# KV sums as row-pair matmuls into two PSUM banks, in a one-core gated attention and MLP kernel

## The chip, the cores and the metric

The kernel runs on one core of one Trainium2 chip. The metric is device time in microseconds, lower is better. Times are medians over single executions. The profile is of one execution, and its span is about 2 us shorter than the time measured for the same execution. Kernels are compared only within the same rounds.

## The reference, cut to what matters

```python
# x: (1, 2048, 448), bf16; 16 heads of 28
q, k, v = split(x @ wqkv)                        # per head
phi_k = concat(softmax(k @ w_phi), softmax(-(k @ w_phi)))   # phi_q likewise
kv  = einsum("bhsf,bhsd->bhfd", phi_k, v)        # the KV sums: over all 2048 tokens
z   = einsum("bhsf->bhf", phi_k)
a   = ((phi_q @ kv) / (phi_q @ z + 1e-6)) @ wo
b   = gelu(x @ w1 + b1) @ w2 + b2
out = g * a + (1 - g) * b                        # g = sigmoid(x . gate_w)
```

The change concerns `kv` and `z`: one sum over all tokens for eight pairs of heads.

## The kernel before

It is one program without loops; TensorE goes through projections, the hidden layer of the MLP (`hp`), in whose midst the KV sums (`acc`) are put, then the attention's numerators (`nm`) and the output layer (`y`). The sums are 128 matmuls, each over 128 tokens with 58 moving columns (columns of the operand that streams through the array), all summed in one bank of PSUM, the memory that matmuls write:

```python
    def kv_sum(acc, u):
        for t in (2 * u, 2 * u + 1):
            for x in range(NPR):                       # 8 pairs of heads
                nc.tensor.matmul(acc[:, 0, x * (PW + 2):(x + 1) * (PW + 2)],   # 58 columns
                                 lhsT=phik[:, t, x, :, :].rearrange("p s w -> p (s w)"),
                                 rhs=vaug[:, t, x, :], start=(t == 0 and x == 0),
                                 stop=(t == NT - 1), skip_group_check=True)

    def kv_out(acc):
        nc.vector.tensor_tensor(out=KV[:], in0=acc[...], in1=mask[...], op=ALU.mult)   # cut

    for n in range(2 * NJ):                            # 28 units of the hidden layer
        m_unit(n // NJ, n % NJ)                        # 14 matmuls, 64 rows each, in row pairs
        if n < 8:
            q_norm(n)                                  # VectorE sums, GpSimd multiplies, SP transposes
        # ... loads of b2 (n == 5) and w2 (n == 8), cut
        if n == 4:
            acc = wide("acc")
            for u in range(8):
                kv_sum(acc, u)
            kv_out(acc)
            gates()
```

A matmul that reads partitions 0 to 63 uses the upper half of the array's rows, one that reads 64 to 127 the lower half, and two such can run at once: in the trace the two matmuls of such a pair start 4 ns apart. `m_unit` is written that way; `kv_sum` is not.

The softmax here doesn't subtract the row's maximum and nothing guards it: scores larger than these inputs give would overflow.

## Time and profile before

| | before |
|---|---|
| time, median (range), 3 runs | 149.19 us (149.14 to 149.22) |
| span of the profile | 147.5 us |
| TensorE busy | 143.4 us |
| first hp matmul to first nm matmul, by their starts | 46.25 us |

The lines of the page and of the views that carry the argument stand in the prediction.

### The profile page before, as it was taken

The page shows a single profiled execution, that of the slowest core. Times are in us where ns is not written, and L with a number is a line of the kernel's source. Part 1 is how long each engine was busy: PE and PEld are TensorE (multiplying, and loading weights), DVE is VectorE, ACT ScalarE, POOL GpSimd, SP SyncE. Part 2 cuts the span into 40 slices and gives each one's busy share as a digit, 9 for nine tenths or more (in the row PEclk, how much of TensorE's full clock was granted, in tenths as well). Part 3 has the DMA queues.
Part 4 walks back from the last instruction along what each step waited for, and adds up shares of the span by engine and source line. Part 5 has one row for each costly group of instructions (what it writes and reads, how often), then busy time and mean ns, then how long its engine had stood idle before and what let it go on. Part 6 is the DMA issues. An engine that isn't in the chain of part 4 may idle for free.

```text
span 147.5 us, 3138 instructions
## 1 busy us (share of the span) xinstructions
PE 143.4 (97%) x1302; PEld 75.0 (51%) x1302; DVE 87.9 (60%) x139; ACT 75.2 (51%) x91; POOL 68.4 (46%) x49
## 2 busy tenths in 40 slices
PE   7999999999999999999999999999999999999992
PEld 2665544555544854444444445554555455555462
DVE  2353699999999999999300017765665245550312
ACT  1654999989889436767677774000621021111100
POOL 7999999899977999919950000000000000000000
PEclk9999999999999999999999999999999999999999
DMA  4999999999700089982999913333433012225011
GB/s 142 227 215 193 168 195 222 218 220 214 160 2 2 4 144 131 226 169 47 126 158 201 351 66 71 71 76 73 129 98 76 31 62 67 67 67 71 31 62 31
DMA packets 44928, 18.02 MB, mean 122 GB/s; under 512 B 36785, under 2 KB 44914, under 8 KB 44914
## 3 DMA queue, kind: packets, MB, share of 16 engines
q1 hardware_dynamic: 43698, 17.16, 56.5%
q10 hardware_dynamic: 1152, 0.65, 1.6%
q8 instruction: 10, 0.16, 0.5%
q14 instruction: 4, 0.03, 0.1%
q0 software_dynamic: 64, 0.01, 0.0%
HBM read 6.28 MB, written 1.84 MB: 55 GB/s over the span
## 4 chain that ended last, share of the span: by engine, by line
PE 91%; DMA 4%; SPq 2%; DVE 1%; issue 0%
PE y L515 29%; PE hp L463 29%; PE pq L346 7%; PE y L520 6%; DMA WqT<-in_A_wqkv_dram 4%; PE v_ps L330 4%; PE pk L338 4%; PE pk L231 3%; PE acc L353 3%; PE nm L476 3%; SPq L146 2%; PE v_ps L231 2%; PE y L525 1%; PE w_ps L262 1%; PE pk L218 1%; SPq L134 1%
## 5 line engine op out<-in xcount | busy, mean ns | idle before, releaser
L515 PE MATMUL y<-w_sb,gel 128*128 128x448 bf16 (+2 forms) x238 | 45.2, 342 | 0.0
L463 PE MATMUL hp<-xT,w_sb 64*128 64x512 bf16 x196 | 42.6, 376 | 0.0
L463 PE MATMUL hp<-xS,w_sb 64*128 64x512 bf16 x196 | 42.6, 376 | 0.0
L468 ACT ACTIVATE gel<-hp,b1T 128x1024 bf16<-128x1024 f32 x28 | 30.8, 1110 | 13.2 <-PE hp L463 13.2
L515 PEld LDWEIGHTS <-gel 128*128 128x128 bf16 x238 | 22.3, 98 | 20.0 <-issue 0.9
L538 ACT ACTIVATE b2u<-b_sb,ungate 128x448 f32<-128x448 bf16 x16 | 10.2, 666 | 40.8 <-DVE res L530 40.8
L463 PEld LDWEIGHTS <-w_sb 64*128 64x128 bf16 x392 | 19.0, 94 | 23.0
L306 POOL TENSOR_TENSOR phik<-phik,rec 128x1792 bf16<-128x1792 bf16 (+1 forms) x8 | 24.9, 3126 | 1.8 <-DVE rec L303 1.7
L480 DVE TENSOR_SCALAR den<-nm,einv 128x16 f32<-128x16 f32 x16 | 3.7, 230 | 27.9 <-PE nm L476 27.9
L530 DVE SCALAR_TENSOR_TENSOR res<-y,ungate,b2u 128x448 bf16<-128x448 f32 (+2 forms) x17 | 10.8, 653 | 15.4 <-PE y L525 10.1
L301 DVE TENSOR_REDUCE sums<-phik 128x64 f32<-128x1792 bf16 x8 | 16.0, 2000 | 3.2 <-ACT phik L292 3.2
L306 POOL TENSOR_TENSOR oT<-oT,rec 128x1792 bf16<-128x1792 bf16 x4 | 12.7, 3212 | 1.1 <-DVE rec L303 1.1
L520 PE MATMUL y<-wo_sb,oT 128*128 128x448 bf16 (+2 forms) x51 | 11.7, 341 | 0.0
L346 PE MATMUL pq<-Wpq,xT 64*128 64x448 bf16 x56 | 11.5, 349 | 0.0
L346 PE MATMUL pq<-WqS,xS 64*128 64x448 bf16 x56 | 11.4, 349 | 0.0
L306 POOL TENSOR_TENSOR w_sb<-w_sb,rec 128x1792 bf16<-128x1792 bf16 x3 | 9.6, 3212 | 3.0 <-DVE rec L303 3.0
L483 DVE TENSOR_TENSOR o_tok<-nm,den 128x448 bf16<-128x448 f32 x16 | 10.0, 624 | 0.6
L303 DVE RECIPROCAL rec<-sums 128x64 f32<-128x64 f32 x16 | 8.8, 553 | 1.4
L200 DVE CAST vaug<-v_ps 128x896 bf16<-128x896 f32 x7 | 7.5, 1071 | 2.0 <-PE v_ps L212 1.6
L291 ACT ACTIVATE phik<-pk 128x896 bf16<-128x896 f32 x8 | 7.6, 947 | 1.9 <-PE pk L220 1.9
L301 DVE TENSOR_REDUCE sums<-oT 128x64 f32<-128x1792 bf16 x4 | 7.9, 1981 | 0.0
L292 ACT ACTIVATE phik<-pk 128x896 bf16<-128x896 f32 x8 | 7.7, 958 | 0.0
(113 smaller groups left out, 173.6 us busy)
## 6 DMA issues: line engine op xcount, KB each, us to landing
w_sb<-in_B_w_dram SPq DMA_DIRECT2D x4, 784.0 KB, 11.5
out_dram<-res SPq DMA_DIRECT2D x15, 112.0 KB, 1.8
w_sb<-in_B_w_dram SPq DMA_DIRECT2D x2, 448.0 KB, 4.8
w_sb<-in_B_w_dram SPq DMA_DIRECT2D x2, 336.0 KB, 3.7
xS<-xT SPq DMA_DIRECT2D x2, 256.0 KB, 3.5
EqT<-in_A_x_dram ACTq DMA_DIRECT2D x1, 448.0 KB, 3.2
xS<-xT SPq DMA_DIRECT2D x2, 192.0 KB, 3.5
wo_sb<-in_A_wo_dram SPq DMA_DIRECT2D x1, 336.0 KB, 16.9
```

The source lines that it names most:

```text
L292: nc.scalar.activation(out=dst[:, :, :, 1, 0:PW], in_=src, func=ACT.Exp, scale=-1.0)
L301: nc.vector.reduce_sum(out=sums[:], in_=ph, axis=AX.X)
L303: nc.vector.reciprocal(out=rec[:], in_=sums[:])
L306: eng.tensor_tensor(out=ph[:, lo:hi], in0=ph[:, lo:hi], in1=rec[:, lo:hi, :, None].to_broadcast([P, hi - lo, 2, DH]), op=ALU.mult)
L346: nc.tensor.matmul(pq[:, i, 0:D], lhsT=x_half(i, k, h)[:, r * P:(r + 1) * P], rhs=w_half(Wpq, WqS, i, k), start=(k == 0), stop=(k == NK - 1))
L463: nc.tensor.matmul(hp[:, i, :], lhsT=w1_sb[i * HP:(i + 1) * HP, k, j * P:(j + 1) * P], rhs=x_half(i, k, h), start=(k == 0), stop=(k == NK ...
L468: nc.scalar.activation(out=gel[h][:, j, :], in_=hp[:].rearrange("p a b -> p (a b)"), func=ACT.Gelu_apprx_tanh, bias=b1T[:, j:j + 1])
L483: nc.vector.tensor_tensor(out=o_tok[:, t % 4, 0:D].rearrange("p (x h d) -> p x h d", x=NPR, h=2), in0=nmv[:, :, 0:PW].rearrange("p x (h d) ...
L515: nc.tensor.matmul(y, lhsT=gel[t // 8][:, j, (t % 8) * P:(t % 8 + 1) * P], rhs=w2_sb[:, j, cols], start=(opens and j == 0), stop=False)
L520: nc.tensor.matmul(y, lhsT=oT[:, c, t * P:(t + 1) * P], rhs=wo_sb[:, c, cols], start=False, stop=(closes and c == 2))
L530: nc.vector.scalar_tensor_tensor(out=res[:, cols], in0=y, scalar=ungate[:, t:t + 1], in1=b2u[t][:, cols], op0=ALU.mult, op1=ALU.add)
L538: nc.scalar.activation(out=b2u[t][:], in_=b2_sb[:], func=ACT.Copy, scale=ungate[:, t:t + 1])
```

## The change

Intent: the sums get the same 64-row shape as their neighbours, so that TensorE no longer changes its tiling (how its rows are divided among matmuls), and the halves, each in a bank of its own, are added by VectorE. To make room for `total`, `b2u` loses a buffer. Separately a small load on GpSimd moves ahead of three small operations.

```diff
+    nc.gpsimd.dma_start(wphi[0:64, 3, :], wphi_rows[384:448, :])
     nc.gpsimd.memset(hmask[:], 1.0)
     ... two affine_select on hmask ...
-    nc.gpsimd.dma_start(wphi[0:64, 3, :], wphi_rows[384:448, :])
@@ kv_sum
-                nc.tensor.matmul(acc[:, 0, x * (PW + 2):(x + 1) * (PW + 2)],
-                                 lhsT=phik[:, t, x, :, :]..., rhs=vaug[:, t, x, :], ...)
+                for i in range(2):
+                    rows = slice(i * HP, (i + 1) * HP)
+                    nc.tensor.matmul(acc[:, i, x * (PW + 2):(x + 1) * (PW + 2)],
+                                     lhsT=phik[rows, t, x, :, :]..., rhs=vaug[rows, t, x, :], ...)
@@ kv_out
+        halves = [acc[:, i, 0:NPR * (PW + 2)] for i in range(2)]
+        total = work.tile([P, NPR * (PW + 2)], F32, name="total", bufs=1)
+        nc.vector.tensor_copy(out=total[:], in_=halves[0])
+        nc.vector.tensor_tensor(out=total[:], in0=total[:], in1=halves[1], op=ALU.add)
         nc.vector.tensor_tensor(
-            out=KV[:], in0=acc[:, 0, ...],
+            out=KV[:], in0=total[:]...,
@@ b2_tile
-        b2u[t] = work.tile([P, D], F32, name="b2u", bufs=3)
+        b2u[t] = work.tile([P, D], F32, name="b2u", bufs=2)
```

More of the change, by code (lines that the diff above doesn't have):

```diff
@@ L352, in kv_sum @@
             for x in range(NPR):
-                nc.tensor.matmul(acc[:, 0, x * (PW + 2):(x + 1) * (PW + 2)],
-                                 lhsT=phik[:, t, x, :, :].rearrange("p s w -> p (s w)"),
-                                 rhs=vaug[:, t, x, :], start=(t == 0 and x == 0),
-                                 stop=(t == NT - 1), skip_group_check=True)
+                for i in range(2):
+                    rows = slice(i * HP, (i + 1) * HP)
+                    nc.tensor.matmul(acc[:, i, x * (PW + 2):(x + 1) * (PW + 2)],
+                                     lhsT=phik[rows, t, x, :, :].rearrange("p s w -> p (s w)"),
+                                     rhs=vaug[rows, t, x, :], start=(t == 0 and x == 0),
+                                     stop=(t == NT - 1), skip_group_check=True)
     def kv_out(acc):
+        halves = [acc[:, i, 0:NPR * (PW + 2)] for i in range(2)]
+        total = work.tile([P, NPR * (PW + 2)], F32, name="total", bufs=1)
+        nc.vector.tensor_copy(out=total[:], in_=halves[0])
+        nc.vector.tensor_tensor(out=total[:], in0=total[:], in1=halves[1], op=ALU.add)
         nc.vector.tensor_tensor(
-            out=KV[:], in0=acc[:, 0, 0:NPR * (PW + 2)].rearrange("p (x w) -> p x w", x=NPR),
+            out=KV[:], in0=total[:].rearrange("p (x w) -> p x w", x=NPR),
             in1=mask[:, None, :].to_broadcast([P, NPR, PW + 2]), op=ALU.mult)
```

## The prediction

> **What bounds the kernel now.** I read the page in this order: busy shares, slices, chain, then the stretches of the chain around the KV sums, then the engines that read the sums. The first lines settle which engine matters.
>
> ```profile
> span 147.5 us, 3138 instructions
> PE 143.4 (97%) x1302; PEld 75.0 (51%) x1302; DVE 87.9 (60%) x139; ACT 75.2 (51%) x91; POOL 68.4 (46%) x49
> ...
> PE   7999999999999999999999999999999999999992
> ...
> PEclk9999999999999999999999999999999999999999
> ...
> PE 91%; DMA 4%; SPq 2%; DVE 1%; issue 0%
> ```
>
> TensorE (PE) is busy in every slice after the first, at full clock, and 91% of the chain that ended last is its work. So a change counts only if it alters how long the string of matmuls takes, or opens a hole in it. The measured time is 149.19 us; the span of the profile is 147.5, and I carry differences over one to one.
>
> The chain in order of time shows the piece that the change rewrites, with its neighbours:
>
> ```profile
> 41.23 7.55 PE hp L463 x70
> 48.78 3.75 PE acc L353 x128
> 52.53 1.61 PE hp L463 x13
> ```
>
> 128 matmuls cost 3.75 us, 2.5% of the span, and both neighbours are the hidden-layer matmuls (hp), which already run as pairs on 64 rows each. The timeline of PE at both borders (start, length, then the instruction) shows the seams:
>
> ```profile
> 48.40 0.38 PE L463 MATMUL hp<-xS,w_sb 64*128 64x512 bf16 x1
> 48.40 0.38 PE L463 MATMUL hp<-xT,w_sb 64*128 64x512 bf16 x1
> 48.71 0.46 PE L353 MATMUL acc<-vaug,phik 128*128 128x58 bf16 x10
> ...
> 52.02 0.50 PE L353 MATMUL acc<-vaug,phik 128*128 128x58 bf16 x12
> 52.46 0.39 PE L463 MATMUL hp<-xT,w_sb 64*128 64x512 bf16 x1
> ```
>
> Three readings. (a) The two hp matmuls on different rows start together (48.40 twice; 4 ns apart in the records), and 70 of them take 7.55 us, 0.216 us a pair, which is the time of one: pairing on the row halves works, at 512 columns. (b) The first acc matmul starts 0.31 us after the last hp pair instead of 0.216: about 0.10 us is lost where the matmuls go from 64 to 128 rows. At the other border the last acc starts at 52.336 by its record and hp at 52.458, 0.12 us instead of one acc slot, again nearly 0.10 us lost. (c) A slot of acc: 12 matmuls in 0.50 us, each 0.190 long, give (0.50-0.19)/11 = 28 ns; over all 128 the starts run from 48.713 to 52.336, 3.623/127 = 28.5 ns. The view of the line adds that the weight loads stood still once before the first:
>
> ```profile
> L353 PEld LDWEIGHTS <-phik x128: 95/98/99, 48.7 to 52.3; 128*128 128x128 bf16 x128
> L353 PE MATMUL acc<-vaug,phik x128: 187/190/201, 48.7 to 52.3; 128*128 128x58 bf16 x128
> its engine sat idle before it (us, times) until:
>   issue: 0.4, 1
> ```
>
> 58 columns do not set the 28.5 ns: the matmuls with one moving column in the gate's turn (4.99 to 5.07 us) follow each other at 26 to 28 ns too, also each with its own weight load. A fixed step of load plus matmul sets it.
>
> **What the Trainium skill says.** "TensorEngine Tiling (Array Packing)", Key Properties: changing the tiling mode, not just the tile, drains TensorE. The trace agrees: the 0.10 us at each seam in (b). Same page, Instruction Overhead: about 60 cycles for each matmul, and "Don't take tiling factor from a dimension that's already small". With 58 moving columns this is a direct warning; nothing in the trace before has short matmuls in row pairs, so it neither agrees nor differs. "TensorE: Matmul & The Clock Gate", The mechanism (of row and column tiling): matmuls on different row groups start about 4 ns apart, and a weight load is pulled ahead where row groups differ. The trace agrees: 3 to 4 ns between the partners of hp, for the loads and for the matmuls. "SBUF — State Buffer", Who interferes with whom: a VectorE (DVE) instruction with two SBUF inputs contends with a GpSimd (POOL) instruction that reads SBUF, and the later one is blocked to the end of the first. The trace agrees: at 43.83 POOL's multiplication over half the usual elements took 2.54 us, where whole ones take 3.21, beside a 1.09 us VectorE multiplication with two SBUF inputs.
>
> **The change, part by part.** (1) The KV sums: 128 matmuls over 128 tokens become 256 over 64 tokens, with 256 weight loads for 128, into two PSUM banks. Order on the engine: load, matmul for rows 0 to 63, load, matmul for rows 64 to 127, as in hp. The cost is 128 times the slot s of a pair.
> Before, from the last hp pair ahead (48.40) to the first behind (52.46): 4.06 us. After: 0.216 + 128 s; both seams are gone, as neighbours and sums are then all of 64 rows. This breaks even at s = 30.0 ns. If the partners overlap fully, each half runs its own chain of load and matmul at 28.5 and s is 28.5 to 29: 0.216 + 128 x 0.029 = 3.93, 0.13 us gained. If the second partner's 4 ns are added to every slot, s = 33 and 4.44: 0.38 lost. I take s = 30 as the middle: 0.0. The first hp pair after the present seam also takes 10 ns more than its 213; that is the size of what else is there to gain.
> (2) The sums leave PSUM by three VectorE operations for one. The present one (128x464 from PSUM) takes 577 ns. I estimate the copy and the addition at 0.6 each, by that row. The multiplication with the mask then reads two SBUF operands, so by the contention above it can wait for POOL:
>
> ```profile
> 57.47 0.58 DVE L359 TENSOR_TENSOR KV<-acc,mask 128x464 bf16<-128x464 f32 x1
> 57.97 2.26 DVE L448 TENSOR_SCALAR eL<-eL 128x16 f32<-128x16 f32 x1
> 60.26 3.14 DVE L450 TENSOR_SCALAR ungate<-eL 128x16 f32<-128x16 f32 x1
> 63.43 0.25 DVE L451 RECIPROCAL ungate<-ungate 128x16 f32<-128x16 f32 x1
> ```
>
> Two operations on 16 elements take 2.26 and 3.14 us: they sit behind POOL's 3.2 us multiplications, which end at 60.2 and 63.4. Now the mask multiplication comes up at 57.47 + 1.2 = 58.7, waits until 60.2, and ends at about 60.7; POOL's next one, pushed by 0.5, ends near 63.9; the first small operation waits for it, the second finds POOL without work. VectorE goes on about 0.7 us later than now (63.7 to 64.4), and the later query normalisations with it. Their end frees the space for the second layer's weights, issued at 79.2 and landed from 82.7 to 86.1, while the first matmul that reads them starts at 87.8 and the last part is read near 89.7. Slack 3.6 to 5 us against 0.7: hidden, 0.0. KV itself is first read at 87.3.
> (3) The wphi load goes ahead of POOL's three hmask operations: issued at about 1.5 for 2.2, landed near 5.7 for 6.4 by its present 4.2 us. Its reader on VectorE starts at 6.85, after the other wphi load landed at 6.75; and the PE reaches those products only at 9.1, then waits for WqT, landed at 10.46, whose chain has no POOL work. hmask comes 0.76 us later (3.0), far ahead of 6.85. 0.0.
> (4) b2u has two buffers for three. It is read by the closing operation of each tile. Where four tiles close at once (102.8 to 105.8) ScalarE's 0.67 us and VectorE's 0.68 us alternate and the fourth already starts at 105.78, behind an output transfer; at the end, b2u of tile 15 would be ready near 140.2 and is read at 144.0. 0.0.
> Sum: s alone decides; -0.1 to +0.4 around about 0.0, taken a hair below: 149.1 us.
>
> **The rivals.** Serial short matmuls: the 26 to 28 ns are paid by every load with its matmul, whatever rows it takes. Then s = 2 x 28.5 = 57: 0.216 + 7.3 = 7.5, 3.45 us lost, 152.6. The page's warning speaks for it, and that one column costs as much as 58. Against it: load, load, matmul, matmul after a seam start within 8 ns (52.454 to 52.462). But those stood ready in the queue; a long run of them is not shown.
> Supply of instructions: now 256 instructions go in 3.6 us, 14 ns each; 512 need 7 ns each. The PE's instructions come in 10 packets of 16 KB (256 instructions) over the run, and the one at 50.6 took 1.3 us. Two such packets' worth are now used in 3.8 us. If a refill takes some 2 us from its call, one hole of 0.1 to 0.5 us could open; if decoding itself can't go under 10 ns, s = 40 and 1.3 us are lost. Nothing in the trace is denser than 13 ns for long, so this stays open.
> VectorE's longer path reaching the PE: needs over 3.6 us of delay where I find 0.7; it would show as a PE wait at 88, some tenths of a us. Unlikely.
> All won, s under 28: the weight loads of half height are no shorter in the records (94 against 95 to 98 ns), so I see no source; at best 0.3 us.
>
> **Range and chances.** s from 28 to 34 (probability about 0.65) gives 149.0 to 149.8; a hole or slower supply, s to 38 (0.15 to 0.2), up to 150.4; serial (0.1) 152.6. Range 148.8 to 150.4. Two per cent is 2.98 us: only the serial rival reaches it. Faster 0.01, same 0.89, slower 0.10.
>
> **What would show it.** The first seam: acc starting 0.21 to 0.22 us after the last hp pair, no idle of the loads ahead of it, and the chain's acc piece at 3.6 to 4.2 us with 256 matmuls; 7.3 would be the serial rival, 4.5 to 5.5 with holes the supply. The mask multiplication at about 2 us with its wait, VectorE at 64.4 for the next sums, w2's landing before 87.5. The start unchanged: WqT's products at 10.5. No new wait at the closings. Wrong for me would be s over 34, or any shift ahead of 41 us.

## The result, and the profile after

The changed kernel took 150.16 us (149.84 to 150.66, 4 runs) against 149.20 (149.14 to 149.24) in the same rounds: ratio 1.0067, 95% interval 1.0039 to 1.0096. A ratio is the mean time of one kernel's fast runs over that of the other's of the same rounds, so not quite the ratio of the two medians. The change costs about 1.0 us, less than the 2% of a verdict: "same", and slower all the same. The profiled execution was the slowest of the four, 150.66.

The chain of the changed kernel in order of time (start, length, what), over the stretch that the prediction showed of before:

```profile
41.35 7.55 PE hp L469 x70
48.91 2.64 PE acc L355 x185
51.55 1.18 issue
52.73 1.18 PE acc L355 x71
```

185 matmuls of the sums run, then nothing for 1.18 us for which the profile shows no wait ("issue"), then the other 71. Without the hole the sums would take 2.64 + 1.18 = 3.82 us by this view, where 3.75 stood before. The timeline of TensorE at the borders:

```profile
48.53 0.38 PE L469 MATMUL hp<-xS,w_sb 64*128 64x512 bf16 x1
48.53 0.38 PE L469 MATMUL hp<-xT,w_sb 64*128 64x512 bf16 x1
48.75 2.80 PE L355 MATMUL acc<-vaug,phik 64*128 64x58 bf16 x185
52.73 1.18 PE L355 MATMUL acc<-vaug,phik 64*128 64x58 bf16 x71 [1.18 <-issue]
53.74 0.37 PE L469 MATMUL hp<-xT,w_sb 64*128 64x512 bf16 x1
```

The seam has gone: the first sum starts 0.22 us after the last hp pair, where it was 0.31. And the pairs are as quick as hoped: the starts of the 185 matmuls run from 48.747 to 51.366, and 2.619 us over 92 steps of a pair is 28.5 ns, exactly the slot of one 128-row matmul before. By the starts the hole is 52.731 - 51.366 = 1.365 us; the view's 1.18 counts from the end of the last matmul.

VectorE behind the sums did what was worked out for it. The mask multiplication takes 1.94 us, most of it a wait, the first small operation waits in its turn, the second does not, and the next sums come at 64.45:

```profile
57.60 0.58 DVE L363 COPY total<-acc 128x464 f32<-128x464 f32 x1
58.22 0.64 DVE L364 TENSOR_TENSOR total<-total,acc 128x464 f32<-128x464 f32 x1
58.89 1.94 DVE L365 TENSOR_TENSOR KV<-total,mask 128x464 bf16<-128x464 f32 x1
60.75 3.18 DVE L454 TENSOR_SCALAR eL<-eL 128x16 f32<-128x16 f32 x1
63.96 0.17 DVE L456 TENSOR_SCALAR ungate<-eL 128x16 f32<-128x16 f32 x1
```

w2's last part landed at 87.63, with w2's first reader at 89.1 and the reader of that part some 1.9 us later; nothing waited. The stretch from the first hp to the first nm grew from 46.25 to 47.40 us. From the first pk matmul to the first hp it is 29.62 us in both, and from the first nm to the end 60.23 and 60.24. So the sums have all of the loss. In front of pk the profiled start differs by 0.13 us (11.44 and 11.58); more on that below.

What is the hole? In the window of the DMA traffic from 50.0 to 51.4 us there is a single packet, of the queue that brings TensorE its instructions (16 KB, 256 instructions):

```profile
q8 instruction: 1, 0.02, 5.6%
```

The trace's list of packets has it from 50.095 to 51.357. TensorE started its last matmul before the hole at 51.366, and went on at 52.731, 1.37 us after the packet had landed. That is my theory's ground: **the sums now use up 256 instructions in 1.82 us, and TensorE ran out of instructions**, since the next 256 are called for only about when the ones before them begin to be used (that packet began 0.55 us after the first instruction of the block before the hole had started, at 49.547). The rivals: the pairs themselves stall (the two banks, the row halves, or a late `phik` tile), or the small parts and VectorE do harm.

### The profile page after: what moved, and what is told of

Its sections match the earlier page's. It is cut to its first block, busy times and chain, and to the rows that moved or that the text cites. A ratio compares the mean times of both kernels' runs of the same rounds, so it can differ in the third digit from the quotient of the medians.

```text
span 148.8 us, 3396 instructions
## 1 busy us (share of the span) xinstructions
PE 143.3 (96%) x1430; PEld 75.8 (51%) x1430; DVE 88.5 (59%) x141; ACT 75.3 (51%) x91; POOL 68.8 (46%) x49
## 4 chain that ended last, share of the span: by engine, by line
PE 90%; DMA 3%; SPq 3%; issue 1%; DVE 1%
PE y L521 29%; PE hp L469 28%; PE pq L346 7%; PE y L526 6%; PE v_ps L330 4%; PE pk L338 4%; DMA WqT<-in_A_wqkv_dram 3%; PE pk L231 3%; PE acc L355 3%; PE nm L482 3%; SPq L146 2%; PE v_ps L231 2%; PE y L531 1%; PE w_ps L262 1%; PE pk L218 1%
## 5 line engine op out<-in xcount | busy, mean ns | idle before, releaser
L469 PEld LDWEIGHTS <-w_sb 64*128 64x128 bf16 x392 | 20.0, 94 | 21.9
L486 DVE TENSOR_SCALAR den<-nm,einv 128x16 f32<-128x16 f32 x16 | 3.7, 230 | 28.5 <-PE nm L482 28.5
```

Of the source, the lines that this page charges most:

```text
L469: nc.tensor.matmul(hp[:, i, :], lhsT=w1_sb[i * HP:(i + 1) * HP, k, j * P:(j + 1) * P], rhs=x_half(i, k, h), start=(k == 0), stop=(k == NK ...
```

## The experiments

Each was compared with the reference and correct. "Stretch" is from the start of the first hp to that of the first nm, out of the trace. The first four ran on one chip (kernel before: 149.31, 148.89 to 149.75), the other four on another (149.22, 148.70 to 149.41); on these chips the kernel before varies more between executions than on the first. All ratios below lie within 2%; what differs clear of noise is read from the intervals.

**1. The same sums, spread out** (`e1_spread_pairs`): the changed kernel, its burst cut in eight.

```diff
         if n == 4:
             acc = wide("acc")
-            for u in range(8):
-                kv_sum(acc, u)
+        if 4 <= n < 12:
+            kv_sum(acc, n - 4)
+        if n == 11:
             kv_out(acc)
             gates()
```

> The changed kernel with the KV sums cut in eight: after each of the hidden-layer units 4 to 11, the 32 row-pair matmuls of two token tiles. Same instructions, no dense run of 512. Theory 'instruction supply' (the PE ran out of instructions once, for 1.37 us, because 256 of them went in 1.8 us and the next packet of 256 takes over 3 us from its call to its use): no hole over 0.4 us on the PE anywhere in the sums, the sums cost 128 x 28.6 = 3.66 us, no seams, time 149.0 (149.2 less about 0.15), a ratio to before of 0.998 to 1.000. Rival 'the pairs themselves stall' (PSUM banks, row halves, data waits): a hole or slow slots remain, time 149.9 to 150.6.

Measured: 148.84 us (148.53 to 149.13), ratio 0.9969 (0.9949 to 0.9989). Its chain:

```profile
48.55 0.45 PE acc L355 x32
49.00 1.51 PE hp L469 x14
50.51 0.45 PE acc L355 x32
```

Eight visits of 0.45 to 0.46 us, 3.64 in all, no hole, and each hp unit between them 1.51 us as everywhere. Stretch 46.04: 0.21 less than before, the two seams. So the pairs don't stall, and this version is faster than the kernel before (its interval lies below 1), and so than the changed one (whose intervals lie above 1). The ratio lies below the expected 0.998 to 1.000: the medians differ by 0.47 us, more than the 0.21 that the traces explain; 0.21 us is a ratio of 0.9986, inside the interval, and I claim no more than that.

**2. The same spreading with 128-row sums** (`e2_spread_full`): the kernel before with the same edit of the schedule.

> The kernel before with the same cut in eight, sums still over 128 rows. Theory: each visit pays two seams of 0.095 to 0.105 us, seven visits more than before, so 7 x 0.2 = 1.4 us more: 150.6 us, ratio 1.009 to 1.010. Rival 'the seam is an accident of the first matmul's wait for data' : no seam at the visits without such a wait, time 149.2 to 149.5.

Measured: 150.72 us (150.35 to 151.20), ratio 1.0099 (1.0073 to 1.0125); stretch 47.74, which is 1.49 above before, 0.213 for each of the seven extra visits.

```profile
49.03 0.56 PE acc L353 x16
49.60 1.62 PE hp L463 x14
51.21 0.56 PE acc L353 x16
```

From the start of the last hp matmul to that of the first acc matmul it took 308 or 309 ns at each of the eight visits (211 to 213 with the row pairs of run 1), whether the view has the weight loads' idle time ended by an operation of GpSimd (two visits) or by nothing that it shows (six). The rival for the seam falls. Spreading is cheap only for sums of the neighbours' shape: that is what the row pairs are worth, 0.21 us a visit.

**3. The burst two units later** (`e3_burst_n6`): the changed kernel with `n == 6` for `n == 4`.

> The changed kernel with the whole burst (256 pairs' matmuls in a row) moved two hidden-layer units later, 56 PE instructions. Theory 'instruction supply': the hole stands at a fixed count of PE instructions, the 1206th recorded, so it now comes after 157 of the 256 matmuls where it came after 185; its size 1.0 to 1.4 us; an instruction packet lands within 1.5 us before the PE goes on. Rival 'data or PSUM': the hole stays after matmul 185 (token tile 11, which has no wait of its own) or goes.

```profile
51.69 2.25 PE acc L355 x157
53.94 2.19 issue
56.12 2.57 PE acc L355 x99
```

After 157 matmuls, as the count of instructions said; a hole bound to data would have stayed at 185. (Weight loads and matmuls counted from zero in order of start, the last one before the hole is number 1206 in both.) The size was a miss: 2.38 us by the starts. The instruction packet, which here ran beside other DMA traffic, took 1.78 us where it took 1.26, and landed at 54.704; TensorE went on 1.42 us later. And there is a second loss: from their start to the next hp matmul the 99 remaining matmuls took 2.37 us, where 28.5 ns a pair make 1.41, and the three hp pairs behind them took 0.50 us more than usual. The view by stretches tells why (columns: stretch and its length; busy time and count of PE, PEld, DVE, ACT, POOL; granted clock; DMA share and GB/s):

```profile
53.94:56.12 2.18, 0.00 (x0) 0.00 (x0) 2.08 (x3) 0.00 (x0) 2.18 (x1) 1.00 0.44 85
56.12:58.70 2.58, 2.58 (x101) 2.52 (x102) 2.48 (x3) 0.00 (x0) 2.58 (x2) 0.50 1.61 140
```

The clock of TensorE was halved after the hole, for 3.41 us by the clock's record, from 56.124 on. Stretch 49.88 = 46.04 + 2.38 + 1.47 for the slow clock (0.97 + 0.50 as above), to 0.01. The single look took 152.9 us.

**4. The small parts alone** (`e4_small_parts`): the kernel before with the wphi load moved and two buffers for b2u.

> The kernel before with only the small parts of the change: the wphi load first on GpSimd, two buffers for b2u. Theory: nothing, 149.2, ratio 0.999 to 1.001, WqT's products starting between 10.4 and 10.6 us. Rival 'the earlier load delays the transposing loads' (the changed kernel's start stood 0.13 us later in its profile): WqT's products at 10.6 or later in every run and ratio 1.001 or more.

Measured: 149.43 us (149.16 to 149.59), ratio 1.0008 (0.9990 to 1.0025), stretch 46.26. Nothing to be seen. In its profile the first pk matmul starts at 10.99 us, the second earliest of all ten; over all profiles it lies between 10.90 and 11.70, whatever the kernel. So the 0.13 us by which the changed kernel's start was later says nothing. That the start of WqT's products would lie between 10.4 and 10.6 was a miss, on the early side.

**5. The burst cut once** (`e5_two_bursts`): 128 matmuls after unit 4, 128 after unit 5.

> The changed kernel with its burst cut once: 128 matmuls after hidden-layer unit 4, 128 after unit 5, so 1.5 us of slow hidden-layer matmuls lie between. Theory 'instruction supply': the 256 PE instructions ahead of the 1206th now take 1.0 + 1.5 + 0.6 = 3.1 us instead of 1.8. The two holes seen ended 3.6 us (1.37 us hole) and some 4.6 us (2.38 us hole, a slow packet) after the queue reached the 950th; so a hole of 0 to 0.7 us, after matmul 171 or 172, and none elsewhere. From the first hidden-layer matmul to the first nm: 46.05 us and the hole. Rival 'a burst of pairs has its own limit, whatever is between': the hole stays at 1.0 us or more, or stands elsewhere.

```profile
48.42 1.82 PE acc L355 x128
50.24 1.51 PE hp L469 x14
51.75 1.82 PE acc L355 x128
```

No hole; 149.08 us (148.85 to 149.38), ratio 0.9996 (0.9979 to 1.0014), stretch 46.04. (The 3.6 and 4.6 us of the expectation were reckoned from an earlier moment; by the recorded starts they are 3.2 and 4.2.) One unit of slow matmuls between was enough, though barely: from instruction 950 to 1206 it took 3.13 us, and the packet landed at 50.750, 1.43 us before 1206 was due.

**6. The burst much later** (`e6_burst_n12`): `n == 12`.

> The changed kernel with the burst after hidden-layer unit 12 (224 PE instructions later). Theory 'instruction supply, in blocks of 256': the block border inside the burst that has 256 dense instructions ahead of it is now the 1462nd, 1206 + 256, so the hole comes after 201 or 202 matmuls, and none at the 1206th (which comes after 73 of them, its block having been fetched long before). Size 1.0 to 2.4 us; the PE goes on 1.3 to 1.5 us after an instruction packet lands. Rival 'fixed place in the burst' : after 157 to 185; rival 'only that place of the program': a hole at the 1206th.

```profile
60.50 2.87 PE acc L355 x201
63.37 1.75 issue
65.12 0.96 PE acc L355 x55
```

After 201 matmuls, at instruction 1462 = 1206 + 256, and no hole at 1206. The hole is 1.93 us by the starts; the packet ran from 62.227 to 63.585, and TensorE went on 1.53 us after it. One look, 150.62 us; stretch 47.97 = 46.04 + 1.93.

**7. The changed kernel again** (`e7_changed_again`).

> The changed kernel once more, on the same chip as the others, for a second look at its hole. Theory: the hole at the same instruction (the 1206th, after matmul 185), of 1.0 to 2.4 us, set by when its packet lands plus 1.4 us; from the first hidden-layer matmul to the first nm 46.05 us and the hole (47.40 in the first profile). Ratio to before 1.005 to 1.012. If the hole were an accident of one run: another place, or none.

Measured: 150.12 us (149.68 to 150.71), ratio 1.0065 (1.0044 to 1.0086). The same place, another size:

```profile
48.51 2.64 PE acc L355 x185
51.15 1.42 issue
52.57 1.18 PE acc L355 x71
```

By the starts 1.60 us, stretch 47.64 = 46.04 + 1.60; the packet landed at 51.279, 1.29 us before TensorE went on. The hole's size varies from run to run, and the changed kernel's times spread over 0.8 to 1.0 us in both of its sets. That the one causes the other I have not shown: only two of its ten executions were kept as profiles. Less the 0.21 us of the seams, their holes make 1.15 and 1.39 us, where the medians differ from before by 0.96 and 0.90; both (150.66 and 150.49) were among the slower of their sets.

**8. VectorE's part alone** (`e8_two_banks`): the changed kernel, but with 128-row sums, even token tiles into the first bank, odd ones into the second.

```diff
-                for i in range(2):
-                    rows = slice(i * HP, (i + 1) * HP)
-                    nc.tensor.matmul(acc[:, i, ...], lhsT=phik[rows, t, x, :, :]..., rhs=vaug[rows, t, x, :],
-                                     start=(t == 0 and x == 0), stop=(t == NT - 1), ...)
+                nc.tensor.matmul(acc[:, t % 2, ...], lhsT=phik[:, t, x, :, :]..., rhs=vaug[:, t, x, :],
+                                 start=(t < 2 and x == 0), stop=(t >= NT - 2), ...)
```

> The change's VectorE part and small parts alone: sums over 128 rows as before, even token tiles into one bank, odd ones into the other, added by VectorE. Theory: hidden. VectorE's next sums start at 64.3 to 64.5 (63.7 before), from the first hidden-layer matmul to the first nm 46.25 us as before, time as before, ratio 0.999 to 1.002. Rival 'VectorE delays the PE': a PE wait near 87 us, 0.2 us or more.

Measured: 149.01 us (148.86 to 149.18), ratio 0.9991 (0.9975 to 1.0007), stretch 46.25. The mask multiplication again took 1.94 us. VectorE's next sums started at 63.78, below what I had expected, because this execution's start was 0.54 us earlier; with that taken off they are 0.61 later than before. No PE wait near 87 us. Hidden.

All stretches together: with 128-row sums in one burst 46.25 (before, 4 and 8: 46.25 to 46.26); with pairs 46.04, plus the hole, plus the slow clock where the hole was long. The terms add up to within 0.01 us in every profile.

## Why the prediction was right or wrong

The time fell in the range (148.8 to 150.4, measured median 150.16), and "same" was the likeliest of the three outcomes. The point, 149.1, was 1.1 us low, and that the range held is in part luck: its upper end was reckoned for slots of up to 38 ns, which did not come, while the hole that came was put at no more than 0.5 us, which with the slot of 30 ns gives only 149.7.

- **The seams**: about 0.10 us each, both gone. Right: 0.21 us together in runs 1 and 2.
- **The slot of a pair**: I took 30 ns and called 28.5 to 29 the case of full overlap. It was 28.5. The sums by themselves gain the 0.21 us, where the prediction put 0.0. I took the skill's advice on small dimensions for a direct warning; that reads it too widely, since the change divides the 128 rows and not the 58 columns. No loss came: two short matmuls cost what one cost. (A slip without effect: an hp pair's usual step is 216 ns in the records, not 213.)
- **The rival of serial short matmuls** (s = 57, 152.6 us): it did not come. Nor did the limit of 10 ns for decoding one instruction (s = 40): 256 went in 1.82 us, 7.1 ns each.
- **The supply of instructions**: here is the error, and it is one of size. The prediction named the mechanism, and put it at "one hole of 0.1 to 0.5 us", from "some 2 us" between a refill's call and its use. Four holes measured 1.37, 1.60, 1.93 and 2.38 us. From the start of the first instruction behind one border to the first behind the next it took 3.2, 3.4, 3.8 and 4.2 us where TensorE had to wait. From the border to the landing of the packet were 1.8, 2.1, 2.2 and 2.8 us of it, so "some 2 us" was about right for that; it left out what passes between the landing and the first instruction behind the hole: 1.3 to 1.5 us in all four. With 3.2 us for 2, the sum of that paragraph would have been 3.2 - 1.8 = 1.4 us, and the prediction 149.19 - 0.21 + 1.4 = 150.4. It also had the chance of it at 0.15 to 0.2. Its sign for this case, 4.5 to 5.5 us for the chain's acc piece with holes, came true: 2.64 + 1.18 + 1.18 = 5.00. The packets of the kernel before could have hinted at the lead that is needed; I did not compare their times with the counts of instructions far enough.
- **VectorE's path**: a 2 us mask multiplication (1.94), the next sums 0.7 us later (0.73 in the first profile, 0.61 in run 8), hidden. Right. w2 landed at 87.63 and not before 87.5, 1.5 us later than in the kernel before where 0.7 was reckoned: the transposes in front of it were pushed too (the first four of `w_sb` took 10.43 us for 9.47).
- **The wphi load and b2u**: 0.0 each. Right, by run 4. The load itself landed at 5.24 for 5.7.
- **Faster at best by 0.3 us, "I see no source"** beyond the seams: run 1's 0.21 by the traces fits.

What stays open: why a landed packet takes 1.3 to 1.5 us more, and when exactly a refill is called for. The runs show packets, not calls: those before the four holes began 0.55 to 1.14 us after the start of the block before, and run 1's for the same border 0.75 us ahead of it.

## What to carry to other kernels

Here row pairs took the seams beside their neighbours away and each pair took no longer than the one matmul before (28.5 ns), but they doubled the instructions in the same time. So ask of every dense run how long 256 instructions last: 1.8 us left a hole each time, 3.13 us with slower matmuls in between left none (run 5), and where TensorE had to wait, a block took 3.2 to 4.2 us. A stretch that shows "issue" in the chain, whose place moves by the count of instructions when the program in front of it grows, in steps of 256, and that follows the landing of an instruction packet, is a shortage of instructions, not a data wait. Once the pairs had the shape of their neighbours, spreading them was free, and that version took 0.9969 of the time of the kernel before (148.84 us), where the changed kernel took 1.0065 to 1.0067.

## What the Trainium skill lacked or had wrong

- "Runtime: NRT & Kernel Launch", Instruction fetch mechanics: the page says that instructions arrive in blocks of 16 KiB (256), the next one fetched while the current one is executed, and that the cost of crossing a border is "mostly hidden". The blocks agree (holes at instructions 1206 and 1462, 256 apart; packets of 16 KB). The cost is not hidden for TensorE in a dense run of short matmuls: 1.37, 1.60, 1.93 and 2.38 us. I had not looked this section up before predicting. It lacks a figure of the lead: here a block took 3.2 to 4.2 us where TensorE waited, 1.3 to 1.5 us of it after the packet had landed, and one that lasted 3.13 us left no hole.
- "TensorEngine Tiling (Array Packing)", Instruction Overhead: the page gives an overhead for each matmul, and doesn't say whether short matmuls on different row halves pay it side by side. Here they did: two 64-row matmuls of 58 columns took 28.5 ns together, the same as one of 128 rows.
- The same page, Key Properties: it says that a change of tiling mode drains TensorE, without a size. Here a visit, one change in and one out, cost 0.21 us.
- "TensorE: Matmul & The Clock Gate", What's actually happening: it gives an idle window of about 3.4 us before the clock is halved. In one profile a hole of 2.4 us was followed by half the clock for 3.41 us, and that cost 1.47 us more; holes of 1.4 to 1.9 us were not followed by it. In the clock's record that halving comes after 51.20 us of full clock, 15 times 3.413 us, so changes may fall on a grid of that step; TensorE was idle for 2.2 us of the step before it, and for 1.7 us of the step in run 6 that was not followed by half the clock. One profile of each is no threshold.
